# Attention with packed queries and a gated two-layer product: token halves of 288 over pairs of PSUM banks in place of 512 tokens and a tail of 64

## Chip, cores and metric

The kernel runs on one core of one Trainium2 chip. The metric is device time in microseconds (us) of one execution. Times are medians of the timed runs; the profile is one execution of each kernel. A profile's "span" goes from its first to its last instruction and is some 2 us shorter than the device time of the same execution.

In the profiles PE is TensorE (PEld its weight loads), DVE is VectorE, ACT is ScalarE, POOL is GpSimd, SP is SyncE, and SPq and the like are queues of DMA issues. L142 is line 142 of the kernel that the profile belongs to, so line numbers differ between kernels.

## Reference

```python
# q, k, v: 8 batch elements x 8 heads x 576 tokens x 64;  p: 8 x 8 x 32 x 64 ("packed" queries)
def sm_attn(qq, kk, vv):                     # softmax attention
    s = scale * np.matmul(qq, kk.transpose(0, 1, 3, 2))
    ...
    return np.matmul(a, vv)
p_packed = sm_attn(p, k, v)                  # 32 packed keys per head
out = sm_attn(q, p_packed, p_packed)         # 576 tokens over 32 packed keys
x = out as (8*576 tokens, 512)
h = x @ w_in                                 # 512 x 2048
g = h * np.cos(h)
return g @ w_out                             # 2048 x 512 -> out (4608, 512), float32
```

## The kernel before

One stage per batch element, eight in all. In stage s the kernel computes, for the 576 tokens of element s, the 16 chunks of `h` (128 columns of the 2048 each), their gates `h * cos(h)`, and between them three kinds of other work: the output matmuls of element s-1 (the "filler"), the second softmax of element s+1, and the first softmax of element s+2, which needs k of s+2 transposed. "Gate 15" below is the last gate of a stage; its end on VectorE is used as the end of the stage.

`w_in` is first multiplied into the packed result (`PPW`, called a packed-key piece below, four pieces of 512 columns for each element), so that `h` comes directly from the softmax weights `a2n`.

The parts that the change and the argument touch, with cuts marked by `...`:

```python
work = tc.tile_pool(name="work", bufs=5, space=PSUM)   # five single banks for everything but ...
t_ps = tc.tile_pool(name="t_ps", bufs=1, space=PSUM)   # ... the tails of 64 tokens
o_ps = tc.tile_pool(name="o_ps", bufs=2, space=PSUM)   # and the output matmuls
...
def load(n, b):                       # float32 -> bf16 loads are issued by GpSimd; 2 buffers per tensor
    t = x[n, b] = ld_pool.tile([KP, H, KC * D], BF16, name=n + "_bf", tag=n)
    G.dma_start(out=t, in_=src[n][b]...)
...
def dma_T(n, b):                      # DMA transpose, in SyncE's queue
    t, f = T_tile(n, b)
    nc.sync.dma_start_transpose(out=t, in_=f)
...
def ppw_piece(b, ns, engs):           # a packed-key piece: two banks, one copy of each
    ...
        ps = [work.tile([128, 512], FP32, name="ppw", tag="w") for _ in range(2)]
    ...
                if engs[g] is A:
                    A.activation(out=dst, in_=ps[g], func=AF.Copy, scale=s)
                else:
                    engs[g].tensor_scalar(out=dst, in0=ps[g], scalar1=s, scalar2=None, op0=ALU.mult)
...
def h_mm(b, fc):                      # 2 matmuls of 512 tokens, and the tails of 64 gathered in one bank
    ps = h_open[b, fc] = work.tile([128, 512], FP32, name="hT", tag="w")
    for g in range(2):
        nc.tensor.matmul(ps, h_lhs(b, g, fc), a2n[b][:, g, 0:512], ...)
    j = fc % 8
    for jj in {2: (0, 1), 3: (2, 3)}.get(j, (j,) if j > 3 else ()):
        ...
            nc.tensor.matmul(ht[b][:, jj, :], h_lhs(b, g, fc - j + jj), a2n[b][:, g, 512:576], ...)

def h_sin(b, fc):
    cs = cos_pool.tile([128, 512], BF16, name="cosT")
    A.activation(out=cs, in_=ps, func=AF.Sin, bias=pihalf)
    todo = [lambda: V.tensor_tensor(out=gT[b][:, fc, :], in0=ps, in1=cs, op=ALU.mult)]
    if fc % 8 == 7:                   # eight tails at once; VectorE writes them into joint
        ...
        todo.append(lambda: V.tensor_tensor(
            out=joint[b // 2][:, fc - 7:fc + 1, j0:j0 + 64], in0=tl, in1=ct, op=ALU.mult))
...
for s in range(B):
    ...
    if s > 1 and n2:
        for n in "kqv":
            load(n, s + 2)
        dma_T("k", s + 2)
    ...
    h_steps(s, range(0, mid), before, ...)      # first half of the chunks
    if n1:
        exp_phase(s, mid, s + 1, s + 2 ...)     # second softmax of s+1, first softmax of s+2
    ...
        dma_T("q", s + 2)
    h_steps(s, range(mid, NFC), before, ...)    # second half
```

`joint` holds the last 64 tokens of two batch elements, so that the output matmuls always have 128 rows.

The softmax here doesn't subtract the row's maximum and nothing guards it: scores larger than these inputs give would overflow.

Of the kernel before, what the change touches and what calls it, by code (L numbers as in the profile page):

```python
# [16 lines left out]
def kernel(  # L17
# [23 lines left out]
    KP, KC = 96, S // 96  # L41
# [13 lines left out]
    work = ctx.enter_context(tc.tile_pool(name="work", bufs=5, space=PSUM))  # L55
    t_ps = ctx.enter_context(tc.tile_pool(name="t_ps", bufs=1, space=PSUM))
# [7 lines left out]
    w_out_bf = const.tile([128, NFC, DM], BF16, name="w_out_bf")  # L64
    ident = const.tile([128, 128], BF16, name="ident")
# [14 lines left out]
    def load(n, b):  # L80
        t = x[n, b] = ld_pool.tile([KP, H, KC * D], BF16, name=n + "_bf", tag=n)
        G.dma_start(out=t, in_=src[n][b].rearrange("h (p c) d -> p h (c d)", c=KC))  # L82
# [13 lines left out]


# [10 lines left out]
    def pe_T(n, b, engs, parts=(0, 1, 2)):  # L108
        if 0 in parts:
            pe_T.open[n, b] = T_tile(n, b)  # L110
        t, f = pe_T.open[n, b]
        for i in parts:
            ps = work.tile([128, 8, KP], BF16, name="tps", tag="w")
            for j in range(8):
                nc.tensor.transpose(ps[:, j, :], f[:, (8 * i + j) * 128:(8 * i + j + 1) * 128], ident[0:KP, 0:KP])  # L115
            copy(engs[i % len(engs)], t[:, 8 * i:8 * i + 8, :], ps)

    pe_T.open = {}

    def pack_p(b0, b1):  # L120

        n = 2 * (b1 - b0)
        ps = work.tile([128, n, 4, 32], BF16, name="pps", tag="w")
        for g in range(n):
            nc.tensor.transpose(ps[:, g].rearrange("p h n -> p (h n)"),
                                p_bf[:, 2 * b0 + g].rearrange("p t d -> p (t d)"), ident)
        dst = P2[:, b0:b1].rearrange("p b h t n -> p (b h) t n")
        sv = ps.rearrange("p g h n -> p (g h) n")
        for t in range(2):
            r = slice(64 * t, 64 * t + 64)  # L130
            V.tensor_copy(out=dst[r, :, t, :], in_=sv[r])
# [5 lines left out]
    def s1_mm(b, i):  # L137

        ps = s1_ps[b, i] = work.tile([128, 2, 2, 4, 32], FP32, name="s1", tag="w")
        for h in range(H):  # L140
            x0 = (h * (KC // 2) + i) * KP
            nc.tensor.matmul(ps[:, :, h % 2, h // 2, :], xT["k", b][:, x0:x0 + 128],  # L142
                             P2[:, b, h], start=True, stop=True)

    def s1_exp(b, i):
        ps = s1_ps.pop((b, i))
        A.activation(out=a1T[:, 2 * i:2 * i + 2].rearrange("p c o a n -> p (c o a n)"),  # L147
                     in_=ps[0:KP].rearrange("p c o a n -> p (c o a n)"), func=AF.Exp, scale=scale)

    def pp_piece(b):  # L150
        ps = work.tile([128, 132], FP32, name="pp", tag="w")
# [12 lines left out]
        t = ppT[b] = small.tile([128, H, 32], BF16, name="ppT")  # L164
        tv = t.rearrange("p (a o) n -> p a o n", o=2)
        for o in range(2):
            for half in range(2):
                V.tensor_copy(out=tv[64 * half:64 * half + 64, :, o, :], in_=pv[64 * o:64 * o + 64])  # L168
        rinv[b] = small.tile([128, 4], FP32, name="rinv")
        V.reciprocal(rinv[b], ps[:, 128:132])  # L170

    def ppw_piece(b, ns, engs):
# [3 lines left out]
        opened = []  # L176
        for n in ns:
            ps = [work.tile([128, 512], FP32, name="ppw", tag="w") for _ in range(2)]
            opened.append((n, ps))
            for hp in range(4):  # L180
                for o in range(2):
                    r = slice(64 * o, 64 * o + 64)
                    nc.tensor.matmul(ps[o][32 * hp:32 * hp + 32], ppT[b][r, 2 * hp + o, :],  # L183
                                     w_in_bf[r, hp, n * 512:(n + 1) * 512], start=True, stop=True,
                                     tile_position=(64 * o, 32 * hp))
        for n, ps in opened:
            for g in range(2):
                dst = PPW[b][:, g, n * 512:(n + 1) * 512]
                s = rinv[b][:, 2 * g:2 * g + 1]
                if engs[g] is A:  # L190
                    A.activation(out=dst, in_=ps[g], func=AF.Copy, scale=s)  # L191
                else:
                    engs[g].tensor_scalar(out=dst, in0=ps[g], scalar1=s, scalar2=None, op0=ALU.mult)  # L193

    def s2_mm(b, g):

        ps = s2_ps[b, g] = [work.tile([128, S // 2], FP32, name="s2", tag="w") for _ in range(2)]
        for hp in range(4):
            for o in range(2):
                r = slice(64 * o, 64 * o + 64)  # L200
                h = 2 * hp + g
                nc.tensor.matmul(ps[o][32 * hp:32 * hp + 32], ppT[b][r, h, :],
                                 xT["q", b][r, h * (S // 2):(h + 1) * (S // 2)],
                                 start=True, stop=True, tile_position=(64 * o, 32 * hp))

    def s2_exp(b, g):
# [3 lines left out]
        for o in range(2):  # L210
            A.activation(out=a2u[b][:, g, o * (S // 2):(o + 1) * (S // 2)], in_=ps[o], func=AF.Exp,  # L211
                         scale=rinv[b][:, 2 * g + 1:2 * g + 2])

    def sums(b, i):

        if b not in lns:
            lns[b] = a2_pool.tile([128, 2, S], FP32, name="lns", tag="lns")
        w = 2 * S // 3
        c = slice(i * w, (i + 1) * w)
        ps = work.tile([128, w], FP32, name="sm", tag="w")  # L220
        nc.tensor.matmul(ps, ones_blk, a2u[b].rearrange("p g s -> p (g s)")[:, c], start=True, stop=True)  # L221
        A.activation(out=lns[b].rearrange("p g s -> p (g s)")[:, c], in_=ps, func=AF.Ln)  # L222

    def normalise(b):
        a2n[b] = a2n_pool.tile([128, 2, S], BF16, name="a2n", tag="a2n")
        A.activation(out=lns[b], in_=lns[b], func=AF.Exp, scale=-1.0)  # L226
        for g in range(2):
            V.tensor_tensor(out=a2n[b][:, g], in0=a2u[b][:, g], in1=lns[b][:, g], op=ALU.mult)  # L228
# [5 lines left out]
    gT, joint, ht, h_open = {}, {}, {}, {}  # L234

    def h_lhs(b, g, fc):
        return PPW[b][:, g, (fc // 4) * 512 + fc % 4:(fc // 4 + 1) * 512:4]

    def h_mm(b, fc):


        if fc == 0:
            gT[b] = g_pool.tile([128, NFC, 512], BF16, name="gT", tag="gT")
            if b % 2 == 0:
                joint[b // 2] = g_pool.tile([128, NFC, 128], BF16, name="joint", tag="joint")
        ps = h_open[b, fc] = work.tile([128, 512], FP32, name="hT", tag="w")
        for g in range(2):
            nc.tensor.matmul(ps, h_lhs(b, g, fc),  # L248
                             a2n[b][:, g, 0:512], start=(g == 0), stop=(g == 1))
        j = fc % 8  # L250
        for jj in {2: (0, 1), 3: (2, 3)}.get(j, (j,) if j > 3 else ()):
            if jj == 0:
                ht[b] = t_ps.tile([128, 8, 64], FP32, name="ht", tag="ht")
            for g in range(2):
                nc.tensor.matmul(ht[b][:, jj, :], h_lhs(b, g, fc - j + jj),  # L255
                                 a2n[b][:, g, 512:576], start=(g == 0), stop=(g == 1))

    def h_sin(b, fc):

        ps = h_open.pop((b, fc))  # L260
        cs = cos_pool.tile([128, 512], BF16, name="cosT")
        A.activation(out=cs, in_=ps, func=AF.Sin, bias=pihalf)  # L262
        todo = [lambda: V.tensor_tensor(out=gT[b][:, fc, :], in0=ps, in1=cs, op=ALU.mult)]  # L263
        if fc % 8 == 7:
            tl = ht[b]
            ct = cos_pool.tile([128, 8, 64], BF16, name="cosTt")
            A.activation(out=ct, in_=tl, func=AF.Sin, bias=pihalf)  # L267
            j0 = (b % 2) * 64
            todo.append(lambda: V.tensor_tensor(  # L269
                out=joint[b // 2][:, fc - 7:fc + 1, j0:j0 + 64], in0=tl, in1=ct, op=ALU.mult))  # L270
        return todo
# [4 lines left out]
    def store(b, y0, y1, osb, r):  # L276

        rows = out[b * S:(b + 1) * S, :].rearrange("(p c) d -> p c d", c=KC)
        while y0 < y1:
            i, p0 = y0 // KP, y0 % KP  # L280
            m = min(y1 - y0, KP - p0)
            nc.sync.dma_start(out=rows[p0:p0 + m, 2 * (i % 3) + i // 3, :], in_=osb[r:r + m, :])
            y0, r = y0 + m, r + m

    def out_gen(b):
        chunks = [(gT[b], i) for i in range(4)]
        if b % 2 == 1:
            chunks.insert(0, (joint[b // 2], None))
        for t, i in chunks:
            x0 = 0 if i is None else i * 128  # L290
            ps = o_ps.tile([128, DM], FP32, name="ot", tag="ot")
            for fc in range(NFC):
                nc.tensor.matmul(ps, t[:, fc, x0:x0 + 128], w_out_bf[:, fc, :],  # L293
# [3 lines left out]
            osb = o_pool.tile([128, DM], FP32, name="osb")  # L297
            copy(V if n_out[0] % 2 == 0 else A, osb, ps)
# [20 lines left out]
    def run(todo):  # L319
        for f in todo:  # L320
            f()


    load("k", 0)
    nc.sync.dma_start(out=p_raw[:, 0:6, :], in_=p_rows[:, 0:6, :])
    make_identity(nc, ident)
    load("v", 0)
    load("q", 0)
    load_w_in(0, 512)
    load("k", 1)  # L330
    for n in range(1, 4):
        load_w_in(512 * n, 512 * n + 512)
    load("v", 1)
    load("q", 1)
    load("k", 2)
    G.dma_start(out=p_raw[:, 6:, :], in_=p_rows[:, 6:, :])
# [15 lines left out]
    exp_table()  # L352
    V.memset(P2[:, 0:3], 0.0)
# [8 lines left out]

    dup_p(0, 6, V)
    pack_p(0, 3)
    V.memset(P2[:, 3:], 0.0)


    pe_T("k", 0, [V, A])
    for i in range(3):
        s1_mm(0, i)  # L370
        s1_exp(0, i)
    pp_piece(0)
    pe_T("q", 0, [V, A])
# [3 lines left out]
    ppw_piece(0, [0], [V, V])  # L377
    for i in range(3):
        sums(0, i)
    pe_T("k", 1, [V])  # L380
    normalise(0)
    for i in range(3):
        s1_mm(1, i)
        s1_exp(1, i)


    def h_steps(b, fcs, before, n_fill):

        n_f, n = 0, len(fcs)
# [107 lines left out]
```

## Time and profile before

| | before |
|---|---|
| device time before the change was made | 273.21 us median of 3 runs (273.0 to 274.27) |
| span of the profiled run | 272.8 us |
| PE busy | 252.7 us, 93% of the span |
| ends of gate 15 of stages 0, 1, 5, 7 (timeline of VectorE) | 54.6, 87.0, 201.2, 250.9 us |
| first cosine, first output matmul | 25.86, 55.83 us |

The page of before draws the span in 40 slices of 6.8 us. A digit is the busy share in tenths; PEclk is TensorE's granted clock in tenths of full speed.

```profile
PE   1797878799999999999999999999999999999992
ACT  1357978947978697689977896889786986564000
PEclk9999975769999999999999999999999999999998
```

From about 62 us on PE has no slice below 9 until the end. The clock is reduced only near 35 to 59 us and after the last matmul. So after the start every microsecond is PE's, and a change in the steady stages counts only if it changes PE's work or makes PE wait.

The windows view, cut at the ends of gate 15, gives for stages 2 and 3: from:to, length, busy (and count) of PE, PEld, DVE, ACT and POOL, then the granted clock, the DMA share and GB/s.

```profile
86.90:116.90 30.00, 30.00 (x280) 15.46 (x279) 18.49 (x33) 23.53 (x39) 2.30 (x3) 1.00 0.73 128
116.90:144.00 27.10, 26.94 (x265) 14.04 (x264) 18.17 (x32) 23.56 (x38) 2.30 (x3) 1.00 1.05 169
```

PE is busy for the whole stage at full clock. ACT and DVE have slack.

The groups view puts the tails at 24.3 us (busy time, mean ns of one), and the timeline of PE in the last stage (start, length, engine, line, what, count) shows what they cost:

```profile
L248 PE MATMUL hT<-a2n,PPW 128*128 128x512 bf16 x256 | 79.1, 394 | 2.6 <-DVE gT L263 1.3
L255 PE MATMUL ht<-a2n,PPW 128*128 128x64 bf16 x256 | 24.3, 198 | 0.0
```

```profile
229.79 0.60 PE L248 MATMUL hT<-a2n,PPW 128*128 128x512 bf16 x2
230.22 1.03 PE L293 MATMUL ot<-w_out_bf,gT 128*128 128x512 bf16 x4
231.09 0.59 PE L248 MATMUL hT<-a2n,PPW 128*128 128x512 bf16 x2
231.52 0.30 PE L255 MATMUL ht<-a2n,PPW 128*128 128x64 bf16 x4
231.66 1.03 PE L293 MATMUL ot<-w_out_bf,gT 128*128 128x512 bf16 x4
```

Starts are what to read, since matmuls overlap: from the start of the tails to the next output matmul is 0.14 us for four of them. That is 35 ns each, where the group's mean says 198.

GpSimd's timeline shows when loads are issued (in brackets, the idle time before and what ended it; `issue` there means that the profile shows nothing that was waited for):

```profile
67.16 0.78 POOL L82 DMA_DIRECT2D k_bf<-in_k_dram  x1 [0.93 <-PE tps L115]
95.63 0.77 POOL L82 DMA_DIRECT2D k_bf<-in_k_dram  x1 [12.38 <-DMA kT_106<-k_bf]
```

The first is k of element 5, which is used in stage 3, from 116.9 us. It waits only for a free buffer and runs 50 us ahead. Its transpose, in SyncE's timeline, and the matmul that needs it, in PE's:

```profile
119.04 6.10 SPq L106 DMA_TRANSPOSE kT_107<-k_bf  x1
...
127.22 0.40 PE L142 MATMUL s_2016<-P_102,kT_107 128*128 128x64 bf16 x8
```

The transpose is issued at 119.04 and the key-score matmul starts at 127.22 us; the list of waits shows 0.3 us in which its weight load waited for this transpose. That hand-over has hardly any slack.

### The profile page before, as it was taken

What the parts mean: (1) busy time and instruction counts of PE and PEld (TensorE: products, weight loads), DVE (VectorE), ACT (ScalarE), POOL (GpSimd) and SP (SyncE); (2) the same over time, 40 slices, a digit from 0 to 9 for tenths busy, and PEclk for the clock granted to TensorE, in tenths of its full rate; (3) what the DMA queues carried; (4) which work ended last, traced back from release to release, by engine and by line L of the source; (5) the groups of instructions that cost most, each with busy time, mean ns of one, the idle gap of its engine ahead of it and who ended that gap; (6) DMA issues with size and microseconds to landing.
All of it is one profiled execution on the core that took longest, in us unless ns stands there. A gap on an engine that the chain in (4) does not pass through costs nothing.

```text
span 272.8 us, 5701 instructions
## 1 busy us (share of the span) xinstructions
PE 252.7 (93%) x2352; PEld 135.4 (50%) x2352; DVE 161.2 (59%) x285; ACT 192.3 (70%) x304; POOL 26.8 (10%) x41
## 2 busy tenths in 40 slices
PE   1797878799999999999999999999999999999992
PEld 0655555246554555545554555445544455554440
DVE  5255971878279726684488528781987187565110
ACT  1357978947978697689977896889786986564000
POOL 8431252003002010101020000000000000000000
PEclk9999975769999999999999999999999999999998
DMA  7999999996999991599989318333511121111322
GB/s 114 202 205 206 204 229 206 204 204 91 216 177 161 176 161 45 126 163 181 160 149 211 68 54 121 89 69 92 113 38 41 38 50 57 50 38 42 88 74 70
DMA packets 49194, 33.99 MB, mean 125 GB/s; under 512 B 23488, under 2 KB 43968, under 8 KB 49168
## 3 DMA queue, kind: packets, MB, share of 16 engines
q0 software_dynamic: 21600, 18.68, 44.5%
q1 hardware_dynamic: 27568, 14.95, 25.2%
q8 instruction: 18, 0.29, 0.4%
q14 instruction: 8, 0.07, 0.1%
HBM read 37.22 MB, written 9.44 MB: 171 GB/s over the span
## 4 chain that ended last, share of the span: by engine, by line
PE 82%; ACT 7%; DMA 5%; issue 2%; POOL 1%; DVE 1%; ACTq 0%; POOLq 0%
PE ot L293 47%; PE hT L248 19%; DMA k_bf<-in_k_dram 5%; PE ppw L183 3%; PE ht L255 3%; ACT cosT L262 3%; PE pp L156 2%; PE tps L115 2%; ACT a1T L147 1%; PE sm L221 1%; ACT PPW L191 1%; PE pp L161 1%; ACT L262 1%; ACT a2u L211 1%; DVE gT L263 1%
## 5 line engine op out<-in xcount | busy, mean ns | idle before, releaser
L293 PE MATMUL ot<-w_out_bf,gT 128*128 128x512 bf16 x512 | 133.7, 381 | 0.0
L262 ACT ACTIVATE cosT<-hT,pihalf 128x512 bf16<-128x512 f32 x128 | 86.6, 688 | 42.1 <-PE hT L248 37.9
L263 DVE TENSOR_TENSOR gT<-hT,cosT 128x512 bf16<-128x512 f32 x128 | 86.5, 685 | 31.3 <-ACT cosT L262 31.2
L248 PE MATMUL hT<-a2n,PPW 128*128 128x512 bf16 x256 | 79.1, 394 | 2.6 <-DVE gT L263 1.3
L293 PEld LDWEIGHTS <-gT 128*128 128x128 bf16 x512 | 43.3, 98 | 41.0 <-issue 4.3
L248 PEld LDWEIGHTS <-PPW 128*128 128x128 bf16 x256 | 28.5, 115 | 30.5 <-issue 6.3
L255 PEld LDWEIGHTS <-PPW 128*128 128x128 bf16 x256 | 24.3, 116 | 21.1 <-issue 2.4
L228 DVE TENSOR_TENSOR a2n<-a2u,lns 128x576 bf16<-128x576 bf16 x16 | 11.4, 754 | 36.5 <-ACT lns L226 36.5
L193 DVE TENSOR_SCALAR PPW<-ppw,rinv 128x512 bf16<-128x512 f32 x33 | 24.5, 746 | 5.4 <-PE ppw L183 5.3
L255 PE MATMUL ht<-a2n,PPW 128*128 128x64 bf16 x256 | 24.3, 198 | 0.0
L93 ACT COPY osb<-ot 128x512 f32<-128x512 f32 x18 | 10.6, 589 | 17.0 <-PE ot L293 16.9
L95 DVE COPY osb<-ot 128x512 f32<-128x512 f32 x18 | 12.3, 683 | 15.8 <-PE ot L293 15.8
L191 ACT ACTIVATE PPW<-ppw,rinv 128x512 bf16<-128x512 f32 x31 | 21.1, 682 | 0.0
L183 PE MATMUL ppw<-w_in_bf,ppT 64*32 64x512 bf16 x256 | 15.1, 414 | 1.9 <-DVE gT L263 1.8
L293 PE MATMUL ot<-w_out_bf,joint 128*128 128x512 bf16 x64 | 16.5, 380 | 0.0
L82 POOL DMA_DIRECT2D q_bf<-in_q_dram x8 | 6.2, 776 | 68.8 <-DMA qT<-q_bf 42.5
L168 DVE CAST ppT<-pp 64x128 bf16<-64x128 f32 x32 | 9.2, 286 | 5.0 <-PE pp L161 4.6
L222 ACT ACTIVATE lns<-sm 128x384 f32<-128x384 f32 x24 | 10.9, 504 | 0.8 <-PE sm L221 0.3
L115 PE MATMUL tps<-ident,k_bf 96*128 96x96 bf16 x96 | 7.3, 255 | 4.4 <-DMA k_bf<-in_k_dram 3.4
L269 DVE TENSOR_TENSOR joint<-ht,cosTt 128x512 bf16<-128x512 f32 x16 | 10.9, 680 | 0.0
L267 ACT ACTIVATE cosTt<-ht,pihalf 128x512 bf16<-128x512 f32 x16 | 10.9, 680 | 0.0
L231 ACT ACT_TABLE_LOAD x8 | 10.3, 1283 | 0.9 <-PEq L481 0.7
(160 smaller groups left out, 193.2 us busy)
## 6 DMA issues: line engine op xcount, KB each, us to landing
k_bf<-in_k_dram POOLq DMA_DIRECT2D x8, 576.0 KB, 13.1
v_bf<-in_v_dram POOLq DMA_DIRECT2D x8, 576.0 KB, 10.1
q_bf<-in_q_dram POOLq DMA_DIRECT2D x8, 576.0 KB, 8.8
out_dram<-osb SPq DMA_DIRECT2D x24, 192.0 KB, 2.3
out_dram<-osb SPq DMA_DIRECT2D x24, 128.0 KB, 2.4
w_in_bf<-in_moe_w_in_dram POOLq DMA_DIRECT2D x4, 512.0 KB, 17.1
w_out_bf<-in_moe_w_out_dram POOLq DMA_DIRECT2D x4, 512.0 KB, 20.3
out_dram<-osb SPq DMA_DIRECT2D x24, 64.0 KB, 2.0
```

Of the source, the lines that this page charges most:

```text
L95: eng.tensor_copy(out=out, in_=in_)
L115: nc.tensor.transpose(ps[:, j, :], f[:, (8 * i + j) * 128:(8 * i + j + 1) * 128], ident[0:KP, 0:KP])
L183: nc.tensor.matmul(ps[o][32 * hp:32 * hp + 32], ppT[b][r, 2 * hp + o, :], w_in_bf[r, hp, n * 512:(n + 1) * 512], start=True, stop=True, ti ...
L191: A.activation(out=dst, in_=ps[g], func=AF.Copy, scale=s)
L193: engs[g].tensor_scalar(out=dst, in0=ps[g], scalar1=s, scalar2=None, op0=ALU.mult)
L222: A.activation(out=lns[b].rearrange("p g s -> p (g s)")[:, c], in_=ps, func=AF.Ln)
L228: V.tensor_tensor(out=a2n[b][:, g], in0=a2u[b][:, g], in1=lns[b][:, g], op=ALU.mult)
L248: nc.tensor.matmul(ps, h_lhs(b, g, fc), a2n[b][:, g, 0:512], start=(g == 0), stop=(g == 1))
L255: nc.tensor.matmul(ht[b][:, jj, :], h_lhs(b, g, fc - j + jj), a2n[b][:, g, 512:576], start=(g == 0), stop=(g == 1))
L262: A.activation(out=cs, in_=ps, func=AF.Sin, bias=pihalf)
L263: todo = [lambda: V.tensor_tensor(out=gT[b][:, fc, :], in0=ps, in1=cs, op=ALU.mult)]
L293: nc.tensor.matmul(ps, t[:, fc, x0:x0 + 128], w_out_bf[:, fc, :], start=(fc == 0), stop=(fc == NFC - 1))
```

## The change

Its intent is to give ScalarE and VectorE fewer and larger instructions. Each chunk of `h` becomes two halves of 288 tokens over a pair of banks, so one cosine and one gate cover all 576 tokens and the tails with their bank disappear. The work pool becomes three pairs. GpSimd copies the last 64 tokens into `joint`. The packed keys' sums (`rinv`) no longer scale the copies of `PPW`; they are taken in where `a2n` is normalised. The start gets another order of loads and of packed-key pieces, and warm-up matmuls. The core of the diff, cut:

```diff
-    work = ctx.enter_context(tc.tile_pool(name="work", bufs=5, space=PSUM))
-    t_ps = ctx.enter_context(tc.tile_pool(name="t_ps", bufs=1, space=PSUM))
+    work = ctx.enter_context(tc.tile_pool(name="work", bufs=3, space=PSUM))
...
+    def pair(shape, dtype, name):
+        ...
+        full = work.tile([128, 4096 // mybir.dt.size(dtype)], dtype, name=name, tag="w")
...
+    def warm(n):
+        ps = o_ps.tile([128, DM], FP32, name="ot", tag="ot")
+        for _ in range(n):
+            nc.tensor.matmul(ps[:, 0:256], zeros[:, 0:128], zeros[:, 0:256], start=True, stop=True)
...
     def ppw_piece ...
+        if spare:
+            ps = [o_ps.tile([128, 512], FP32, name="ot", tag="ot") for _ in range(2)]
+        else:
+            full = pair([2, 512], FP32, "ppw")
+            ps = [full[:, 0], full[:, 1]]
...
-                    A.activation(out=dst, in_=ps[g], func=AF.Copy, scale=s)
+                copy(eng[g], dst[:, g], ps[g])
...
     def normalise ...
-            V.tensor_tensor(out=a2n[b][:, g], in0=a2u[b][:, g], in1=lns[b][:, g], op=ALU.mult)
+            V.scalar_tensor_tensor(out=a2n[b][:, g], in0=a2u[b][:, g], scalar=rinv[b][:, 2 * g:2 * g + 1],
+                                   in1=lns[b][:, g], op0=ALU.mult, op1=ALU.mult)
...
     def h_mm ...
-        ps = h_open[b, fc] = work.tile([128, 512], FP32, name="hT", tag="w")
+        ps = h_open[b, fc] = pair([2, 512], FP32, "hT")
         for g in range(2):
+            for o in range(2):
+                nc.tensor.matmul(ps[:, o, 0:HS], w, a2n[b][:, g, o * HS:(o + 1) * HS],
+                                 start=(g == 0), stop=(g == 1))
...
     def h_sin ...
+        def gate():
+            V.tensor_tensor(out=gT[b][:, fc, :]..., in0=ps, in1=cs, op=ALU.mult)
+            if fc % 8 == 7:
+                G.tensor_copy(out=joint[b // 2][:, fc - 7:fc + 1, b % 2, :], in_=gT[b][:, fc - 7:fc + 1, 512:S])
...
-    load_w_in(0, 512)
     load("k", 1)
-    for n in range(1, 4):
+    for n in range(2):
         load_w_in(512 * n, 512 * n + 512)
     load("v", 1)
+    load_w_in(1024, 1536)
     load("q", 1)
     load("k", 2)
+    load_w_in(1536, 2048)
...
         if s == 0:
-            mid = 12
+            mid = 10
             (packed-key pieces 1 to 3 of element 1 move from stage 0 to stage 1; others move too)
```

The lines that issue the loads and the transposes in the steady stages are not touched. The joint chunk of the output matmuls comes third instead of first, and the last output copy is split between two engines.

## The prediction

> **What bounds the kernel now.** The page gives TensorE (PE) 93% of the 272.8 us span. By the stretch view PE is busy essentially all the time from 62 to 268 us. Before that it is not the limit: from 25.9 to 54.9 us (stage 0) ScalarE and VectorE run nearly back to back (timeline), and the granted clock falls to 0.66 at 40 to 60 us. PE's continuous output matmuls begin at 55.8 us; everything later is PE work at 216 ns per 512 columns.
>
> **PE work of the steady stages barely changes.** The 64-column tails look dear in the groups (24.3 us busy), but in the timeline of the last stage a step with four tails takes 1.43 us, with two 1.36, with none 1.30: about 32 ns each. Per 16 chunks: old 32 x 216 + 32 x 32 ns = 7.9 us; new 64 matmuls of 288 columns at about 122 ns (estimate, scaled from 216) = 7.8 us.
>
> **ScalarE and VectorE get cheaper**, mostly off the path: Sin 16 x 688 + 2 x 680 -> 16 x about 742 ns; PPW copies lose their scale (682 -> about 590); the exp phase has fewer, larger activations (-0.9 us). This counts only in stage 0.
>
> **The start gains.** k1 lands ahead of w_in, about 2.5 us earlier than at 19.85; warm-up matmuls should keep the clock (24 transposes took 2.1 us early, 1.05 late). The Trainium skill, "TensorE: Matmul & The Clock Gate", Part 1, says that the clock is gated after about 3.4 us without activity; the trace's 0.66 agrees in kind. My walk puts the first output matmul near 51 us instead of 55.8, with 2.2 us of packed-key work moved behind it. Net start -3.5 us, end (split last copy) -0.5. Three pairs of banks instead of five banks cost about 0.2 us a stage where a query-score matmul waits for a gate.
>
> **The hidden cost: GpSimd's queue.** Before, GpSimd only issues loads after the start, and runs far ahead: k5 is issued at 67.2 us, though its stage begins near 115. Now the joint copy, which waits for the last gate of each stage, stands in that queue ahead of the loads for two stages on. In stages 2 to 5 the k load can be issued only after the previous stage's gate 15 (before: 86.9, 116.8, 144.0, 174.0 us). Add 0.7 us for the copy, 6.2 from issue to landing, then the DMA transpose, 5.0 alone, 8.1 beside loads (q and v now follow directly). The key-score matmuls stand at 98.6, 127.2, 155.7, 184.4, that is 10.4 to 11.7 us after the gate; about 15 are needed. PE stands still 3 to 4.7 us in each of four stages, about 15 us in all (5 if the transposes meet no loads). The before trace already shows one such wait, 0.3 us on kT. Long stalls may also drop the clock.
>
> **Prediction.** 273.2 - 4 (start, end) - 0.7 + 1.5 (banks) + about 13 (stalls, shaded for overlap) = about 283 us. Range 266 to 290. Chances: faster by over 2% 0.17, within 2% 0.15, slower 0.68.
>
> **What would show it.** Right: PE idle before the key-score matmuls (released by a DMA transpose of k) in four stages; k loads issued just after joint copies; first output matmul at 49 to 53 us; step time in the last stage 1.35 us. Wrong: no PE idle from 60 us to the end, and a time near 268.
>
> **What would make it wrong.** Loads and transposes landing faster than 6.2 and 8.1 us; the start gaining far more because the clock stays full; three pairs stalling PE at every packed-key piece; 288-column matmuls limited by their doubled weight loads (+3 us or more a stage).

## The result

After: 315.09 us median (312.99 to 317.44, 4 runs). Before, on the same chip: 273.11 us (272.27 to 274.27, 4 runs). The ratio is 1.154, with a 95% interval of 1.143 to 1.165. Ratios here are the mean time of one kernel's fast runs over that of the other's fast runs of the same rounds, so they are not quite the ratio of the medians. The direction was as predicted; the size was not, and the range of 266 to 290 us did not hold it.

The page of after (slices of 7.8 us) has holes in PE's row that before has not:

```profile
PE   5968786879889499993999649995799999999993
PEclk9997977999999979996899969999599999999999
```

The windows view, cut at the ends of gate 15, for stages 2 and 3, and one window inside stage 3:

```profile
92.80:129.10 36.30, 31.39 (x276) 18.17 (x280) 17.94 (x30) 23.12 (x33) 3.46 (x5) 0.95 0.68 118
129.10:164.80 35.70, 29.43 (x262) 16.95 (x265) 18.04 (x30) 23.03 (x32) 3.53 (x5) 0.90 0.64 113
...
142.90:149.70 6.80, 4.34 (x31) 2.48 (x33) 0.00 (x0) 1.61 (x2) 0.00 (x0) 0.50 0.40 96
```

A stage that had 30.0 or 27.1 us now has 36.3 or 35.7. PE is idle for 4.9 and 6.3 us of it, and in a part of it the granted clock is one half.

The waits of after name the stall (engine, line, for what: us in total, times, longest):

```profile
PE s L159 <- DMA kT<-k_bf: 20.3, 4, 6.2
...
ACT PPW L97 <- DVE PPW L99: 15.4, 27, 1.1
```

One stage of it in detail, GpSimd's timeline first, then SyncE's queue, then PE's:

```profile
129.15 0.61 POOL L275 COPY joint<-gT 128x512 bf16<-128x512 bf16 x1 [25.07 <-DVE gT L273]
130.21 0.78 POOL L85 DMA_DIRECT2D k_bf<-in_k_dram  x1 [0.45 <-PE ppw L202]
130.98 0.77 POOL L85 DMA_DIRECT2D q_bf<-in_q_dram  x1
131.74 0.77 POOL L85 DMA_DIRECT2D v_bf<-in_v_dram  x1
```

```profile
136.50 6.54 SPq L120 DMA_TRANSPOSE kT<-k_bf  x1
```

```profile
137.81 2.12 PE L299 MATMUL ot<-w_out_bf,gT 128*128 128x512 bf16 x9
145.14 1.04 PE L159 MATMUL s<-P,kT 128*128 128x64 bf16 x16 [5.21 <-DMA kT<-k_bf]
146.39 1.49 PE L299 MATMUL ot<-w_out_bf,gT 128*128 128x512 bf16 x3 [0.22 <-issue]
```

The reader is to follow k of element 5, as before. GpSimd stood at the joint copy for 25.07 us until gate 15 of stage 2 was done, at 129.1 us. Only then was k issued, at 130.21, against 67.16 before. It reached its transpose at 136.50 and PE at 145.14, 5.21 us too late. Behind the waiting matmul stood output matmuls with all their data ready. The Trainium skill, "TensorE: Matmul & The Clock Gate", Part 2, says that only weight loads are pulled ahead and that matmuls stay in program order; this trace agrees, since none of the output matmuls ran in those 5.21 us. The last line shows the second cost: three output matmuls took 1.49 us after the stall, where three take 0.81 at full clock.

PE's own work is as predicted. The group and the last stage, as shown of before:

```profile
L263 PE MATMUL hT<-a2n,PPW 128*128 128x288 bf16 x512 | 85.6, 293 | 8.2 <-DVE gT L273 3.9
```

```profile
286.03 0.65 PE L263 MATMUL hT<-a2n,PPW 128*128 128x288 bf16 x4
286.74 0.81 PE L299 MATMUL ot<-w_out_bf,gT 128*128 128x512 bf16 x3
287.38 0.65 PE L263 MATMUL hT<-a2n,PPW 128*128 128x288 bf16 x4
287.87 2.32 PE L299 MATMUL ot<-w_out_bf,gT 128*128 128x512 bf16 x10
```

From 287.38 to 287.87 four matmuls of 288 columns take 0.49 us, 122.5 ns each, and a step is 1.35 us. (The estimate from 216 ns per 512 columns was 122. The Trainium skill, same page, section "Wait — 56ns, not 53.3ns?", gives N / 2.4 GHz and about 2.5 ns more; worked out for 288 and 512 columns that is an estimate of 122.5 and 215.8 ns. The trace agrees: 122.5 here, and a median of 216 from one output matmul to the next in the last stage.)

Where the 38.2 us between the two profiled spans (311.0 and 272.8) came from, by the ends of gate 15 (rounded to 0.1 us):

| part of the span, us | before | after | difference |
|---|---|---|---|
| start to end of stage 1 | 87.0 | 92.8 | +5.8 |
| stages 2 to 5 | 114.2 | 147.1 | +32.9 |
| stage 6 | 28.0 | 28.1 | +0.1 |
| stage 7 | 21.7 | 21.6 | -0.1 |
| last output matmuls and stores | 21.9 | 21.4 | -0.5 |

Stages 6 and 7 have no loads left to wait for, and they changed by less than 0.2 us. In these two stages, at least, halves of 288, pairs and larger gates are neither a gain nor a loss for PE.

### The profile page after: what moved, and what is told of

It is laid out like the page before. It is cut to its first block, busy times and chain, and to the rows that moved or that the text cites. A ratio compares the mean times of both kernels' runs of the same rounds, so it can differ in the third digit from the quotient of the medians.

```text
span 311.0 us, 5737 instructions
## 1 busy us (share of the span) xinstructions
PE 261.1 (84%) x2367; PEld 154.6 (50%) x2398; DVE 160.5 (52%) x269; ACT 186.7 (60%) x260; POOL 37.6 (12%) x59
## 4 chain that ended last, share of the span: by engine, by line
PE 59%; DMA 15%; DVE 11%; ACT 10%; issue 3%; POOL 1%; DVEq 0%; ACTq 0%; POOLq 0%
PE ot L299 33%; PE hT L263 15%; DMA kT<-k_bf 11%; DVE gT L273 5%; DMA k_bf<-in_k_dram 4%; ACT cosT L270 3%; PE s L159 2%; DVE PPW L99 2%; PE ppw L202 2%; PE pp L173 2%; ACT PPW L97 2%; PE tps L127 2%; DVE ppT L99 2%; ACT L270 1%; ACT lns L236 1%
## 5 line engine op out<-in xcount | busy, mean ns | idle before, releaser
L270 ACT ACTIVATE cosT<-hT,pihalf 128x576 bf16<-128x576 f32 x128 | 93.7, 741 | 35.2 <-PE hT L263 33.6
L273 DVE TENSOR_TENSOR gT<-hT,cosT 128x576 bf16<-128x576 f32 x128 | 95.8, 754 | 36.7 <-ACT cosT L270 35.6
L263 PE MATMUL hT<-a2n,PPW 128*128 128x288 bf16 x512 | 85.6, 293 | 8.2 <-DVE gT L273 3.9
L245 DVE SCALAR_TENSOR_TENSOR a2n<-a2u,rinv,lns 128x576 bf16<-128x576 bf16 x16 | 12.4, 815 | 60.1 <-ACT lns L243 60.1
L164 ACT ACTIVATE a1T<-s 96x1024 bf16<-96x1024 f32 (+1 forms) x16 | 12.6, 804 | 29.6 <-PE s L159 29.5
L159 PE MATMUL s<-P,kT 128*128 128x64 bf16 x192 | 11.7, 230 | 20.6 <-DMA kT<-k_bf 20.3
L97 ACT CAST PPW<-ppw 128x512 bf16<-128x512 f32 x27 | 15.8, 585 | 15.4 <-DVE PPW L99 15.4
L159 PEld LDWEIGHTS <-kT 128*128 128x128 bf16 x192 | 10.7, 123 | 26.3 <-DMA kT<-k_bf 22.2
L99 DVE CAST PPW<-ppw 128x512 bf16<-128x512 f32 x27 | 18.5, 684 | 0.6 <-PE ppw L202 0.4
L227 ACT ACTIVATE a2u<-s,rinv 128x576 bf16<-128x576 f32 x16 | 11.0, 736 | 0.6 <-PE s L219 0.5
```

What stands on the lines that cost most here:

```text
L97: A.copy(out=out, in_=in_)
L99: eng.tensor_copy(out=out, in_=in_)
L159: nc.tensor.matmul(ps[:, 2 * j:2 * j + 2, h % 2, h // 2, :], xT["k", b][:, x0:x0 + 128], P2[:, b, h], start=True, stop=True)
L164: A.activation(out=a1T[:, 2 * i:2 * i + 2 * n].rearrange("p c o a n -> p (c o a n)"), in_=ps[0:KP].rearrange("p c o a n -> p (c o a n)"), ...
L227: A.activation(out=a2u[b][:, g].rearrange("p (o t) -> p o t", o=2), in_=ps[:, :, 0:HS], func=AF.Exp, scale=rinv[b][:, 2 * g + 1:2 * g + 2])
L245: V.scalar_tensor_tensor(out=a2n[b][:, g], in0=a2u[b][:, g], scalar=rinv[b][:, 2 * g:2 * g + 1], in1=lns[b][:, g], op0=ALU.mult, op1=ALU.mult)
```

## The experiments

Theories at the outset:

- Queue theory: the joint copy in GpSimd's queue holds the loads back until gate 15, and PE waits for the transposed k (predicted, though with a smaller size).
- Clock theory: the stalls also halve the clock, which makes each dearer than its length.
- Bank theory: three pairs hold back stages 0 and 1 (and a little all others), since three tiles can be open where there were five.
- Copy theory (a rival for the small excess of all stages): ScalarE's half of a packed-key pair waits for VectorE's half.
- Load and order theories: the new order of loads, or that of the packed-key pieces, is at fault in the start.

All twelve runs that were made are told. Parts of the span in one table, in us, from the ends of gate 15 in each profile; the text below refers to it:

| kernel | median time | to end of stage 1 | stages 2 to 5 | span |
|---|---|---|---|---|
| before | 273.11 | 87.0 | 114.2 | 272.8 |
| after | 315.09 | 92.8 | 147.1 | 311.0 |
| e1_hoist | 282.9 | 93.7 | 117.5 | 282.2 |
| e2_joint_dve | 283.96 | 92.4 | 117.8 | 281.2 |
| e3_before_gpjoint | 306.19 | 87.1 | 146.3 | 304.9 |
| e4_hoist_whole | 281.85 | 91.1 | 117.5 | 279.7 |
| e5_five | 271.5 | 81.6 | 116.4 | 269.3 |
| e6_five_oldsched | 278.69 | 90.0 | 115.3 | 276.6 |
| e7_pairs_oldsched | 283.24 | 92.5 | 116.5 | 280.0 |
| e8_before_loads | 278.18 | 91.3 | 114.3 | 277.2 |
| e9_five_early_k | 271.58 | 83.2 | 115.4 | 269.8 |
| e10_stall_warm | 309.99 | 93.4 | 143.7 | 308.1 |
| e11_five_nowarm | 271.86 | 83.6 | 115.3 | 270.2 |
| e12_four | 282.74 | 88.3 | 120.6 | 281.3 |

The kernel before had medians of 274.36 us (e1 to e4), 272.79 (e5 to e8) and 272.68 (e9 to e12) in the same rounds.

### e1_hoist: the loads half a stage earlier

```diff
 (after, with)
         if s > 1 and n2:
-            for n in "kqv":
-                load(n, s + 2)
             dma_T("k", s + 2)
...
             dma_T("q", s + 2)
+        if s > 0 and s + 3 < B:
+            for n in "kqv":
+                load(n, s + 3)
         h_steps(s, range(mid, NFC), before, filler[1])
```

The joint copy stays on GpSimd; only the loads now stand ahead of gate 15's copy in its queue.

> The changed kernel, except that the loads of k, q and v for a stage are issued half a stage earlier, ahead of the joint copy of gate 15. Queue theory (the joint copy holds the loads back): the waits of the key-score matmuls on the DMA transpose of k (20.3 us on PE) fall below 2 us, the clock stays full after 65 us, stages 2 to 5 fall back to about 30 and 27 us each (33 us less in all), total 279 to 286. Rival (three bank pairs and the copies of the two halves of a pair one after the other cost it): the waits go but the time stays above 298.

Measured: 282.9 us (282.11 to 284.57), ratio to before 1.031 (1.025 to 1.037). In the same stage as above, GpSimd's timeline shows k of element 5 issued behind gate 7's joint copy, and PE's clock row has no drop left after the start:

```profile
104.41 0.61 POOL L275 COPY joint<-gT 128x512 bf16<-128x512 bf16 x1 [10.03 <-DVE gT L273]
105.48 0.78 POOL L85 DMA_DIRECT2D k_bf<-in_k_dram  x1 [0.45 <-issue]
```

```profile
PEclk9997997799999999999999999999999999999999
```

No wait of PE for kT is left in stages 2 to 5, which take 117.5 us. The queue block is worth 147.1 - 117.5 = 29.6 us. What remains over before in these stages, 3.3 us, and the start are something else.

### e2_joint_dve: the joint copy on VectorE

```diff
 (after, with)
-                G.tensor_copy(out=joint[b // 2][:, fc - 7:fc + 1, b % 2, :], in_=gT[b][:, fc - 7:fc + 1, 512:S])
+                V.tensor_copy(out=joint[b // 2][:, fc - 7:fc + 1, b % 2, :], in_=gT[b][:, fc - 7:fc + 1, 512:S])
```

> The changed kernel with the joint copy on VectorE in place of GpSimd, loads in their old place in the program. Queue theory: GpSimd runs ahead again as before the change (k5 issued before 75 us), total within 3 us of the run with the earlier loads, 279 to 287. Rival: above 298.

Measured: 283.96 us (2 runs), ratio 1.036 (1.028 to 1.044). The load of k of element 5 is back at 67.53 us (before: 67.16):

```profile
67.53 0.78 POOL L85 DMA_DIRECT2D k_bf<-in_k_dram  x1 [1.58 <-PE tps L127]
```

Two repairs that have nothing in common but the order of GpSimd's queue give the same 117.5 and 117.8 us. It is where the copy stands, not the copy's 0.61 us.

### e3_before_gpjoint: the queue block alone, on the kernel before

```diff
 (before, with)
-            todo.append(lambda: V.tensor_tensor(
-                out=joint[b // 2][:, fc - 7:fc + 1, j0:j0 + 64], in0=tl, in1=ct, op=ALU.mult))
+            jt = cos_pool.tile([128, 8, 64], BF16, name="jt")
+            todo.append(lambda: V.tensor_tensor(out=jt, in0=tl, in1=ct, op=ALU.mult))
+            todo.append(lambda: G.tensor_copy(
+                out=joint[b // 2][:, fc - 7:fc + 1, j0:j0 + 64], in_=jt))
```

> The kernel before, with one thing added: the gated tails go to a small tile and GpSimd copies them into the joint tile, so that each stage's last gate stands in GpSimd's queue ahead of later loads; banks, matmuls and start are as before. Queue theory: this alone costs most of the loss, 22 to 35 us in stages 2 to 5 with a fallen clock in them: total 295 to 308. Rival: 272 to 277.

Measured: 306.19 us (305.51 to 306.98), ratio 1.117 (1.112 to 1.123). The wait and the clock row:

```profile
PE s L142 <- DMA kT<-k_bf: 23.3, 4, 7.3
```

```profile
PEclk9999777699999799995999959999699999999999
```

Start and stages 6 and 7 are before's within 0.1 us. Stages 2 to 5 grew by 32.1 us: 23.3 us of waits, and, as an estimate, half of the 17.1 us that PE worked inside windows of half clock, 8.5 us, which makes 31.8. The queue block alone costs about 32 us without pairs, halves or another load order.

### e4_hoist_whole: a packed-key pair copied by one engine

```diff
 (e1, with)
-        if isinstance(eng, tuple):
+        if isinstance(eng, tuple) and not spare:
+            copy(eng[n % 2], dst, full)
+        elif isinstance(eng, tuple):
```

The reason is this pair of lines from the timeline of after, and the same two copies in stage 0, where each half has a tile of its own:

```profile
122.21 0.69 DVE L99 CAST PPW<-ppw 128x512 bf16<-128x512 f32 x1 [0.17 <-PE ppw L202]
122.93 0.58 ACT L97 CAST PPW<-ppw 128x512 bf16<-128x512 f32 x1 [0.36 <-DVE PPW L99]
```

```profile
26.51 0.58 ACT L97 CAST PPW<-ot 128x512 bf16<-128x512 f32 x1
26.68 0.68 DVE L99 CAST PPW<-ot 128x512 bf16<-128x512 f32 x1
```

Halves of one tile were copied one after the other: by the profile ScalarE's copy waited for VectorE's. Halves in two tiles were copied at the same time, and e5 (below), which gives each half a tile of its own throughout, has no such wait. These are the 15.4 us of the waits above.

> The run with the earlier loads, and the pair of packed-key banks is copied by one engine in one instruction (VectorE and ScalarE in turn), where before ScalarE's half waited 15.4 us in all for VectorE's half of the same pair. If these waits hold up PE through the three pairs: 2 to 5 us under the run with the earlier loads, most of it in stage 1. If not: within 1 us of it.

Measured: 281.85 us (281.65 to 282.41), ratio 1.029 (1.024 to 1.034), against e1's 1.031. The 15.5 us of waiting is gone from the list of waits, and about 1 us of time with it; the intervals overlap. The copy theory is at most a small part: these waits of ScalarE held up PE by 1 us at most.

### e5_five: everything of the change but the pairs

The change's loads, warm-ups, normalisation and order of pieces, on five single banks and a tail bank, with 512 and 64 tokens as before; the tails go to `joint` by VectorE.

```diff
 (after, with)
-    work = ctx.enter_context(tc.tile_pool(name="work", bufs=3, space=PSUM))
+    work = ctx.enter_context(tc.tile_pool(name="work", bufs=5, space=PSUM))
+    t_ps = ctx.enter_context(tc.tile_pool(name="t_ps", bufs=1, space=PSUM))
...
-            full = pair([2, 512], FP32, "ppw")
-            ps = [full[:, 0], full[:, 1]]
+            ps = [work.tile([128, 512], FP32, name="ppw", tag="w") for _ in range(2)]
...
 (h_mm, h_sin, s1, s2 and sums as before)
```

> The changed kernel (its loads, warm-up matmuls, rinv moved to a2n, new order of the packed-key pieces in stages 0 and 1) on the old banks: five single banks, 512 + 64 tokens, tails and joint on VectorE as before. Bank theory (three pairs in place of five banks hold up PE where many kinds of tile are mixed, in stages 0 and 1): total 269 to 274, stage 1 (between the last gates of stages 0 and 1) 33 to 35 us where the pairs with earlier loads need 39. Order theory (the new order of pieces overloads stage 1): stage 1 stays at 37 us or more, total 278 to 283.

Measured: 271.5 us (271.04 to 271.96), ratio 0.993 (0.987 to 0.999). Stage 1 of after, of e5 and of e12 (below) in the windows view:

```profile
54.40:92.80 38.40, 32.98 (x401) 20.23 (x407) 25.04 (x45) 25.03 (x36) 1.23 (x2) 1.00 0.38 70
```

```profile
49.30:81.60 32.30, 30.97 (x396) 17.98 (x395) 24.32 (x48) 25.28 (x42) 3.84 (x5) 1.00 1.15 190
```

```profile
53.10:88.30 35.20, 32.11 (x396) 18.51 (x402) 24.91 (x48) 25.49 (x42) 3.84 (x5) 1.00 1.13 179
```

With the same order of loads and pieces, stage 1 takes 32.3 us on five banks and 38.4 on three pairs, at full clock in both. The waits of PE in after's stage 1 are many and short, for copies and gates that must give back a tile:

```profile
PE s L219 <- ACT PPW L97: 1.1, 1, 1.1
PE pps L141 <- ACT PPW L97: 0.9, 2, 0.6
PE pp L173 <- DVE gT L273: 0.9, 1, 0.9
```

On five banks the end of stage 1 comes at 81.6 us, 5.4 earlier than before's 87.0. On pairs it comes at 92.8. (The profiled run of e5 had no window of half clock in the start, that of before had 17 us of it and that of after 10 us, so part of these differences is luck of the run. e9 and e11, below, have the start of e5, e11 without its warm-up matmuls, and had 6.8 us of it each; their stage 1 ends at 83.2 and 83.6 us. By the timed runs e5 is 0.7% faster than before, 1 to 2 us.) Without the pairs the loss in the start is gone, as the bank theory said. But e5 changes the shapes of the tiles too, so this shows the pairs as a whole to be the cause, and not yet the number of open tiles.

### e6_five_oldsched and e7_pairs_oldsched: the old order of packed-key pieces

```diff
 (e5, and e4, with)
         if s == 0:
-            mid = 10
-            before[1].append(lambda: ppw_piece(0, 1, (V, A), True))
-            before[4].append(lambda: pp_piece(1, (V, A)))
-            ...
+            mid = 12
+            for n in range(1, 4):
+                before[4 * n - 3].append(lambda n=n: ppw_piece(0, n, (V, A), True))
+            before[8].append(lambda: pp_piece(1))
+            ...
```

> The run with the old banks, and also the old order of the packed-key pieces in stages 0 and 1; of the change only the load order, warm-up matmuls, rinv in a2n and the split last copy stay. Bank theory: within 2 us of the run with the old banks, 268 to 274. Order theory: 6 to 9 us under it.

Measured: 278.69 us (277.41 to 280.0), ratio 1.019 (1.012 to 1.025), outside what was expected. Its list of waits has one of 4.0 us of PE for a piece of `w_in` between 15 and 62 us; e5 has none of these. The new order of loads brings the later pieces of `w_in` too late for the old order of packed-key pieces.

> The changed kernel with earlier loads and pairs copied whole (281.9 us) in the old order of the packed-key pieces. Bank theory: 278 to 285, the loss only moves between stages 0 and 1. Order theory: 272 to 276.

Measured: 283.24 us (282.46 to 284.04), ratio 1.035 (1.029 to 1.041), against e4's 1.029 in other rounds. The old order does not repair the pairs' start, but the test is not clean: e7 also waits for `w_in`, 2.4 us, and in both e6 and e7 the pieces of element 1 in stage 0 go to the output banks. The order is not indifferent either. In the old order pairs are 4.5 us behind five banks (e7 against e6), in the new one about 10 (e4 against e5), and stage 1 takes 34.6 and 37.6 us on pairs, 33.0 and 32.4 on five banks.

### e8_before_loads: the new order of loads alone

```diff
 (before, with)
-    load_w_in(0, 512)
     load("k", 1)
-    for n in range(1, 4):
+    for n in range(2):
         load_w_in(512 * n, 512 * n + 512)
     load("v", 1)
+    load_w_in(1024, 1536)
     load("q", 1)
     load("k", 2)
+    load_w_in(1536, 2048)
```

> The kernel before with the new order of loads alone (k1 ahead of w_in). k1 lands about 2.5 us earlier, but the first Sin also waits for w_in: first Sin 0 to 1.5 us earlier, total 271.5 to 274.

Measured: 278.18 us (276.01 to 279.92), ratio 1.016 (1.009 to 1.024): slower, if by less than 2%, and outside what was expected. The first cosine came at 27.22 us, 1.4 us later than in before and not earlier. Its waits between 15 and 60 us:

```profile
PE ppw L183 <- DMA w_in_bf<-in_moe_w_in_dram: 3.9, 2, 2.5
```

The same wait as in e6. The order of loads and that of the pieces are one change: on five banks e5, which has both and the rest of the new start, gains 1 to 2 us (0.4 of it at the end of the span), and the first without the second loses about 5.

### e9_five_early_k: on e5, k of three stages ahead

```diff
 (e5, with)
-        if s > 1 and n2:
-            for n in "kqv":
-                load(n, s + 2)
-            dma_T("k", s + 2)
...
+        if s > 0 and s + 3 < B:
+            for n in "kqv":
+                load(n, s + 3)
         h_steps(s, range(mid, NFC), before, filler[1])
+        if s > 0 and s + 3 < B:
+            dma_T("k", s + 3)
```

> The version with the old banks and the new start (271.5 us), with the loads and the DMA transpose of k for two stages on issued half a stage to a stage earlier. Its one wait for a transposed k, 1.0 us in stage 2, and the slow key-score matmuls of stage 3 (0.4 us) should go: 269.5 to 271 us, the fastest of all.

Measured: 271.58 us (270.96 to 271.64), ratio 0.995 (0.992 to 0.998). This is just outside what was expected. The wait of 1.0 us for kT in stage 2 of e5 is gone (one of 0.2 us stands in stage 3), and stage 2 goes from 31.1 to 30.1 us. But e11 below, with the loads of e5, has no such wait either and the same 30.1 us, so this cannot be put down to the edit. No net gain over e5 can be read.

### e10_stall_warm: after, with PE kept busy ahead of the stall

```diff
 (after, with)
+        if s > 1 and b1 is not None:
+            warm(32)
         for i, n in ((0, 2), (2, 1)):
```

The warm-up matmuls stand just before the key-score matmuls that wait. They fill the stall, so that the clock theory can be told from the wait.

> The changed kernel (315.1 us) with 32 matmuls of zeros (about 3.4 us at full clock) ahead of the key-score matmuls of stages 2 to 5, inside the wait for k, so that PE has work for most of it; the data arrive no sooner. Clock theory (of the 33 us lost in stages 2 to 5, 20 to 22 us are the wait itself and 10 to 12 us the halved clock after it): no clock windows of 0.5 after 65 us, total 303 to 308. Rival (the rest is contention or order, not the clock): 313 to 317.

Measured: 309.99 us (306.82 to 310.27), ratio 1.133 (1.125 to 1.140); the expected range was missed at the upper end. The timeline of PE, two of the four stages:

```profile
110.79 0.64 PE L159 MATMUL s<-P,kT 128*128 128x64 bf16 x16 [1.72 <-DMA kT<-k_bf]
...
181.63 1.03 PE L159 MATMUL s<-P,kT 128*128 128x64 bf16 x16 [3.73 <-DMA kT<-k_bf]
```

The waits left were 1.72, 1.57, 3.73 and 1.93 us. Of the four stages only that with 3.73 lost the clock: the sixteen matmuls after it took 1.03 us, those after 1.72 took 0.64, and the granted clock was 0.50 from 180.0 to 186.8 us and full around the three others. Idle time ahead of PE of 4.1 us or more halved the clock each time in after. The Trainium skill, "TensorE: Matmul & The Clock Gate", Part 1, says that the clock falls to half after about 3.4 us without activity. These runs agree only in part. The waits for kT lie on either side of that figure: those up to 1.93 us kept the clock, those of 3.73 us and more lost it. But in the stage with 3.73 us PE went idle at 177.91 us and the clock was half from 180.0, only 2.1 us later. And in the start of before, where it was half for 17 us, the list of waits from 15 to 62 us has none of PE longer than this:

```profile
PE ppw L183 <- DVE gT L263: 1.8, 1, 1.8
```

So a long stall is not all that costs the clock, and these runs do not show where the limit lies.

The sum over stages 2 to 5, against e1: waits 8.9 us, inserted matmuls 4 x 3.66 = 14.6, half of the 5.0 us that PE worked in the one slow window 2.5, together 26.0, against 143.7 - 117.5 = 26.2 measured. So the clock is a real part, and filling a stall with idle work saves that part only.

### e11_five_nowarm: e5 without warm-up matmuls

```diff
 (e5, with)
     def warm(n):
+        return
```

> The version with the old banks and the new start, without any warm-up matmul. If they keep the clock in the start: windows of half clock come back between 20 and 60 us and stage 0 ends 2 to 5 us later, total 273 to 277. If the order alone does it: within 1 us of 271.5.

Measured: 271.86 us (271.57 to 272.94), ratio 0.997 (0.994 to 1.001). The profile has two windows of half clock of 3.4 us in the start, e5's none, and still the times differ by 0.4 us. e9, with the warm-ups, had 6.8 us of half clock in the start too. On five banks the warm-ups bring nothing that can be measured.

### e12_four: e5 with four banks

```diff
 (e5, with)
-    work = ctx.enter_context(tc.tile_pool(name="work", bufs=5, space=PSUM))
+    work = ctx.enter_context(tc.tile_pool(name="work", bufs=4, space=PSUM))
```

> The version with the old banks and the new start, with four work banks in place of five. Bank theory (how many tiles can be open is what stages 0 and 1 need): last gate of stage 1 later by 2 us or more (81.6 in the run with five), stages 4 to 7 as they were, total 273 to 280. Rival (the loss of the pairs came from their 288-column matmuls or larger instructions): 270.5 to 272.5.

Measured: 282.74 us (282.18 to 283.27), ratio 1.036 (1.033 to 1.040), above the 273 to 280 expected: one single bank costs 11 us (e9, in the same rounds, had 271.58). The end of stage 1 moves by 6.7 us (88.3 against 81.6; 4.7 to 5.1 against e9 and e11, whose profiles had windows of half clock in the start, as this one had), stages 2 to 5 by 4.2 us (120.6 against 116.4) and stage 6 by 1.1; that the later stages suffer too had not been expected. Three pairs lose much less there: e1 has 117.5 us in stages 2 to 5 and nothing lost in stage 6. A pair holds what two single tiles held for scores and packed-key pieces, so three pairs and four single banks are not to be compared by number alone. The wait that appears there is of the query-score matmuls for a tile that a gate must give back; the list of waits from 53 to 240 us has:

```profile
PE s L216 <- DVE gT L281: 4.4, 7, 0.9
```

### A version that beats both

e5 and e9 beat before by 0.7 and 0.5% in the same rounds, and take 14% less than after (271.5 against 315.09 us, in other rounds). No version tried beats before by 2%.

## Why the prediction was right or wrong

The direction and the main mechanism were right. The steps that failed are the sizes of three terms: the stalls, which were costed too short and without the half clock that goes with them, and the pairs of banks, whose cost in the start was left out.

What bounds the kernel was right: PE, and its work did not change. The step of the last stage is 1.35 us as predicted, and stages 6 and 7 are the same within 0.2 us.

The hidden cost was right in kind. The k loads were issued just behind the joint copies in four stages, and PE stood still before the key-score matmuls in the same four. The Trainium skill, "PSUM — Partial Sum Buffer", section "Engine vs sequencer instructions", says that GpSimd's queue is strictly in order; the 25.07 us of idle GpSimd ahead of the joint copy and the loads right behind it agree. e1, e2 and e3 show it from three sides.

The predicted sum was: -4 for start and end, -0.7, +1.5 for banks, +13 for the stalls. Against the profiled runs it missed 38.2 - 9.8 = 28.4 us. By term:

- "PE stands still 3 to 4.7 us in each of four stages, about 15 us in all", shaded to 13. Measured 4.11, 5.21, 6.21 and 4.74 us, 20.3 in all: 7.3 us too few. The shading "for overlap" had no measured reason and was wrong: no output matmul ran in the stall shown above. The rest is in the chain. From gate 15 to the key-score matmul "about 15" was predicted, and 16.2, 16.0, 17.9 and 15.6 us were measured; mostly because loads took 7.4 us on average from k's issue to the start of its transpose, not 6.2 (in before the last three loads of k had taken 11.5, 6.3 and 7.7 us to land). The transposes' 8.1 us was right (8.3 median).
- "Long stalls may also drop the clock" was named but given no microseconds. This term was zero in the sum and about 8.7 us on the chip: in stages 2 to 5 PE worked 17.5 us inside windows of half clock, and half of that is lost (an estimate). Waits and clock together make 20.3 + 8.7 = 29.0 us, and e1 shows 29.6. The before profile already had clocks of 0.66 in the start, and the predicted stalls of 3 to 4.7 us lay around the 3.4 us that the prediction itself quoted. An estimate could have been made blind.
- "Three pairs of banks instead of five banks cost about 0.2 us a stage" is the worst step. Stages 2 to 5 show 3.3 us that e1 leaves; five banks with the rest of the change show 2.2 (e5) and 1.1 (e11) of it, so the pairs' own share is 1.1 to 2.2 us, 0.3 to 0.6 a stage. Stages 0 and 1 show far more: with the same loads and pieces, stage 1 ends at 92.8 us on pairs and at 81.6 to 83.6 on five banks (e5, e9, e11), 9 to 11 us apart. The prediction's own list of what would make it wrong had "three pairs stalling PE at every packed-key piece"; it was not costed.
- "Net start -3.5 us": as a walk of five banks it was not far off (e5, e9 and e11 end stage 1 at 81.6, 83.2 and 83.6, before at 87.0, though luck of the clock is in these figures). With the pairs it became +5.8. The first output matmul came at 53.55 us, just outside the predicted 49 to 53. Of the predicted reasons, the warm-ups are worth nothing that shows on five banks (e11), and the order of loads alone loses time (e8): the gain needs the order of the pieces that goes with it.
- The end: -0.5 predicted, -0.5 measured.

So of the 28.4 us missed, 7.3 are stall length, 8.7 the clock, 2.5 what e1 leaves in the steady stages (3.3 against 4 x 0.2), and 9.3 the start and stage 1 (+5.8 against -3.5); 0.6 is left over. (The prediction's -0.7, for which it gives no reason, and the 0.7 of its 1.5 for banks outside stages 2 to 5 cancel.)

What stays open: how the loss of the pairs in stages 0 and 1 splits. That stages 0 and 1 are sensitive to the number of open tiles is shown by e12, which loses 4.7 to 6.7 us there by one single bank; that it is what the pairs lose by is argued, not shown. The end of stage 1 under e2 excludes the engine of the joint copy (92.4 us), that under e4 leaves little for the paired copies (91.1). That under e7 (92.5) shows that the old order of pieces is no cure, but e6 and e7 together show that the order matters to how much the pairs lose. And e5 also differs from after in the shapes (512 and 64 in place of 288, three score and sum pieces in place of two), and no run separates those from the count.

## What to carry to other kernels

An instruction that waits, put into a queue that has so far only issued loads, turns prefetching into just-in-time loading: before giving an "idle" engine a copy, look in its timeline at how far ahead its loads run, and put the later loads ahead of the copy, or the copy elsewhere. Cost a predicted stall of TensorE by its length and also by the half clock that may follow (here 20.3 and about 8.7 us). Fewer and larger tiles over the same PSUM bytes mean fewer tiles open at once; here they cost 9 to 11 us by the end of the busiest stage, so test them there first. How much of that is the number and how much the shapes was not shown.

## What the Trainium skill lacked or had wrong

- "DMA: Bandwidth & Descriptors", "Latency and other measured facts", gives 261 GB/s for DMA transposes, measured on one kernel, and nothing for a transpose that runs beside loads. By that figure the 0.59 MB of k would take 2.3 us, an estimate. The median from issue to landing of k's transposes was 5.2 us in e1 and 8.3 us in after, where the q and v loads run beside it.
- "PSUM — Partial Sum Buffer" has no cost of having one bank less: e12 shows 11 us of 272 for the fifth work bank.
- No page says that two engines that read the two banks of one PSUM tile are put in order all the same, while two banks in two tiles are read at once: 15.4 us of waits of ScalarE here, 27 times, worth about 1 us (e4).
- "TensorE: Matmul & The Clock Gate", Part 1, ties the half clock to about 3.4 us without activity, which is not all of it: in e10 the clock was half 2.1 us after PE went idle, and in the start of before it was half for 17 us though PE's longest wait there was 1.8 us. The page gives no length for the shorter idles that cost the clock.
